# Unsplit queries for units 8 to 21, TensorE and ScalarE for the residuals of the last weight matrix, and a fourth conversion buffer

## The chip, the cores and the metric

The kernel runs on one core of a Trainium2 chip. The metric is the device time of the whole program in microseconds (us). The kernel before has a median of 1354.19 us over 3 runs (1353.14 to 1354.83).

## What is computed

Top-32 attention followed by two feed-forward layers, all in float32 accuracy:

```python
# attention: 4 batches, 8 heads, 576 positions, head size 64
scores = q @ k.T / 8
kth    = 32nd largest score of each row
attn   = softmax(scores where scores >= kth)
x      = (attn @ v), heads side by side            # 2304 x 512
# layer 1 (w_in 512x2048, w_out 2048x512)
h = x @ w_in
P = a0 + a1*h + a2*h*h + a3*h*h*h
Q = 1 + |b0|*|h| + |b1|*h*h
x = (P / (Q + 1e-6)) @ w_out
# layer 2 (w_in 512x2048, w_out 2048x512)
h = x @ w_in
y = (h * cos(h)) @ w_out                           # 2304 x 512
```

## The kernel before

**Split operands.** The matrix products of the layers use the fast 4-byte format of TensorE (`F32R`), which keeps fewer bits than float32. Each operand is therefore split: a high part (the value copied into `F32R`) and a low part (the value minus the high part), and three products high·high, high·low and low·high are summed. A product that is written with plain float32 operands appears in the profile as two matmul records.

**Weights.** The four weight matrices come in float32 and are split on the chip by `conv` (lines 264 to 312) in 64 pieces of 128x512, 16 of each kind: kind 0 and 1 are layer 1's input and output weights, kind 2 and 3 those of layer 2. The host hands them over as 8-byte words, of which a piece is loaded into a buffer `raw`. Two ScalarE instructions take the words apart into `cb` and the first half of `raw`; VectorE shifts `cb`; GpSimd adds the two (the value is now in `cb`); ScalarE copies it into the high part `h` (a resident tile, or a buffer `ch` for kind 3). Then the difference value minus high part replaces `cb`. It is made in one of three ways: for kinds 0 and 2 (`CPE`) TensorE multiplies the value by the identity and the high part by minus the identity into the PSUM tile `diff`, and ScalarE copies the sum back to `cb`; for kind 3 (`SUBV`) VectorE subtracts; for kind 1 GpSimd subtracts. At last `cb` (for kind 3 also `ch`) is written out by SyncE's DMA queue, and later matmuls stream it back. Buffers of the second phase (kinds 2 and 3): `RB` = 3 of `raw`, `CB` = 3 of `cb`. At most `CD` = 3 conversions are open at a time, and a `cb` buffer is free again only when its write has landed.

**Attention.** The work is 72 units; a unit is 128 query rows of one pair of heads. `qk` (lines 325 to 351) makes the scores of a unit in the PSUM tile `sx` and ScalarE copies them to `sS`; `topk` finds the 32nd largest with VectorE (maximum, minimum, MAX8, MATCH_REPLACE) and masks the exponentials; `av` transposes and multiplies by v. Keys are kept as high and low part stacked on the 128 partitions. Units 0 to 7 multiply the raw float32 q of 64 partitions. From unit 8 on q is split too: `high_q` (ScalarE, before the grouped stage), `low_q` (GpSimd there), and `qk` issues two `F32R` matmuls for each of the 4 score blocks of a unit.

**Order.** The program is written as pieces: piece 5u+p is step p of unit u. Units 0 to 19 (`U0` = 20) and the end are put in order by a scheduler with a timing model of its own, engine by engine; the result is a fixed order on each engine, and an engine whose next instruction waits holds everything behind it. Units 20 to 71 are "grouped": `InOrder` (lines 90 to 117) pins the order that `unit` (lines 877 to 963) writes out by hand. Layer 1 of the first 256 tokens starts at unit 9, and all 64 conversions must be done before the last step of layer 1's first block (line 703). So the conversions of layer 2's weights lie in units 8 to 19, beside attention and layer 1.

In the profile every engine instruction has line 80, the recording helper; tiles tell them apart: `cb<-cb,ch` is the subtraction of kind 3, `cb<-cb` the shift, `cb<-raw` the first ScalarE step, `cb<-diff` the copy from PSUM, `q<-qr` the high part and `q<-qr,q` the low part of q, `sx<-k,q` the split scores, `sx<-kraw,qr` the unsplit ones, `h` and `y` layer 1's products.

Of the kernel before, what the change touches and what calls it, by code (L numbers as in the profile page):

```python
# [10 lines left out]
F32 = mybir.dt.float32  # L11
# [25 lines left out]
NG = NF // 2  # L37
SINB = 2
UA, UB = 9, 18
RA, CA, RB, CB = 5, 6, 3, 3  # L40
PL = 10
P0 = 9
WIN = 8
# [9 lines left out]
WA, PA = 12, 90  # L53
WG, PG = 10, 90
N1, NU, N2, NST, NGG = 1, 2, 2, 4, 3
SUBV = (3,)
CPE = (0, 2)
LAL, LAT = 3, 10
DV1, DV2 = 8, 7
KB, VB, XB = 2, 2, 2  # L60
# [1 line left out]
QRB, QB = 2, 2  # L62
S0 = 46
U0, U1 = 20, 72
C0, C1 = 5 * U0, 5 * U1

ORDER = mybir.DependencyInfo(mybir.DependencyClass.NoSync, mybir.DependencyReason.DATA)
# [52 lines left out]
def body(tc, out, qt, kt, vt, ident_d, w1_d, w1o_d, a_d, b_d, w2_d, w2o_d):  # L120
    nc = tc.nc
    V, A = InOrder(tc, nc.vector, WIN, C0), InOrder(tc, nc.scalar, WA, PA)
    G = InOrder(tc, nc.gpsimd, WG, PG, behind=V)
    PE, SP = InOrder(tc, nc.tensor, 0, 0), nc.sync

    with ExitStack() as ctx:
# [27 lines left out]
        nu = len(units)  # L154
# [38 lines left out]
                qs_[i] = [raw, None]  # L193

        def high_q(i, grouped=False):
            if 8 <= i < nu:
                qs_[i][1] = x = att.tile([P, 2, 2, P], F32R, tag="q", bufs=QB, name=f"q{i}")
                if grouped:
                    G.tensor_copy(x[:, 0], qs_[i][0])
                else:  # L200
                    A.activation(x[:, 0], qs_[i][0], AF.Copy)

        def low_q(i, E):
            if 8 <= i < nu:
                raw, x = qs_[i]
                E.tensor_sub(x[:, 1], raw, x[:, 0].bitcast(F32))

# [56 lines left out]
        def conv(kind, c, x):  # L264
            nm = f"{kind}_{c}_{x}"
            wd = (w1_d, w1o_d, w2_d, w2o_d)[kind]
            src = wd.bitcast(I32).rearrange("(c p) (f t) -> c p f t", p=P, t=2)[c, :, x * CW:(x + 1) * CW, :]
            if kind == 2 and len(whi) == 1:
                tmps.pop().close()
                whi.append(pool("wts2").tile([P, NCC, DF], F32R, name="w2hi"))  # L270
                open_tmp()
            n1, n2 = (RA, CA) if kind < 2 else (RB, CB)
            raw = tmps[0].tmp.tile([P, CW, 2], I32, tag="raw", bufs=n1, name="raw" + nm)
            SP.dma_start(out=raw, in_=src)
            a = tmps[0].tmp.tile([P, CW], F32, tag="cb", bufs=n2, name="cb" + nm)
            lo, hi, ai = raw[:, :, 0], raw[:, :, 1], a.bitcast(I32)
            A.activation(a, hi.bitcast(F32), AF.Prelu, scale=2.0 ** -112, alpha=-2.0 ** 32)
            A.activation(lo, lo.bitcast(U32), AF.Copy, scale=2.0 ** -29)

            def rest():  # L280
                V.tensor_scalar(ai, ai, 3, 0, op0=ALU.logical_shift_left, op1=ALU.bitwise_or)
                G.tensor_add(ai, ai, lo)
                if kind == 3:
                    h = tmps[0].tmp.tile([P, CW], F32R, tag="ch", bufs=2, name="ch" + nm)
                elif kind == 1:
                    h = w1o[:, c, :]
                else:
                    h = whi[kind // 2][:, c, x * CW:(x + 1) * CW]
                A.activation(h, a, AF.Copy)
                if kind in CPE:  # L290
                    if "d" not in diff:
                        diff["d"] = ps_o.tile([P, 2, 512], F32, tag="o", name="diff")
                    diff["n"] = n = diff.get("n", 0) + 1
                    d = diff["d"][:, n % 2]
                    PE.matmul(d, ident, a, start=True, stop=False)
                    PE.matmul(d, nident, h, start=False, stop=True)
                    A.activation(a, d, AF.Copy)
                else:
                    if kind in SUBV:
                        V.tensor_sub(a, a, h.bitcast(F32))  # L300
                    else:
                        G.tensor_sub(a, a, h.bitcast(F32))
                if kind == 3:
                    SP.dma_start(out=w2o[c, :, 0, :], in_=h.bitcast(F32))
                    SP.dma_start(out=w2o[c, :, 1, :], in_=a)
                elif kind == 1:
                    SP.dma_start(out=w1ol[c], in_=a)
                else:
                    dst = wlo[kind // 2][4 * x:4 * x + 4, :, c, :].rearrange("g p t -> p g t")
                    SP.dma_start(out=dst, in_=a.rearrange("p (g t) -> p g t", t=P))  # L310

            return rest
# [8 lines left out]
        def after(mm, bank):  # L321
            for x in order[bank]:
                tc.add_manual_dep(mm.ins, x, mybir.DependencyInfo(mybir.DependencyClass.NoSync, mybir.DependencyReason.DATA), reason="bank")

        def qk(i):
            n, pr = units[i]
            raw, x = qs_.pop(i)
            hi, lo = (x[:, 0], x[:, 1]) if x is not None else (None, None)
            kvs = ins[i]
            m = P // len(kvs)  # L330
            st[i] = sb = att.tile([P, 2, S], F32, tag="sS", bufs=SB, name=f"sS{i}")
            for j in range(2):
                rows = slice(j * D, (j + 1) * D)
                for c, (k, _) in reversed(list(enumerate(kvs))):
                    qs = slice(0, (c + 1) * m)
                    for hf in range(2):
                        o = sx[qs, hf, :HALF]
                        hs = slice(hf * HALF, (hf + 1) * HALF)
                        if n < 2:
                            mm = PE.matmul(o, raw[rows, j, qs], k[rows, 0, hs].bitcast(F32), start=True, stop=True)  # L340
                            after(mm, hf)
                        else:
                            mm = PE.matmul(o, hi[:, j, qs], k[:, j, hs], start=True, stop=False, skip_group_check=True)
                            after(mm, hf)
                            mm = PE.matmul(o, lo[:, j, qs], k[:, j, hs], start=False, stop=True, skip_group_check=True)
                        order[hf] = [mm.ins.name]
                A.activation(halves(sb[:, j]), sx[:, :, :HALF], AF.Copy)
                if j == 0:
                    yield
            if n == 1:  # L350
                store_k(kvs[0][0], 0, pr)
# [417 lines left out]

        def free(i, prev):  # L770
            nq = qk(i + 1) if i + 1 < nu else iter(())
            next(nq, None)
            next(nq, None)
            if i + 2 < nu:
                load_k(i + 2)
            t = topk(i) if i < nu else iter([None] * 9)
            fresh = []
            for p in range(5):
                if p == 0:
                    for x, a in held:  # L780
                        store_k(x, *a)
                    held[:] = [(prep(*a), a) for a in preps.get(i, [])]
                    if prev is not None:
                        next(prev)
                    next(t, None)
                    if prev is not None:
                        next(prev)
                    next(t, None)
                    if prev is not None:
                        a = av(i - 1)  # L790
                        next(a)
                        next(a, None)
                        if i % 4 == 0:
                            nrm.append(norm((i - 1) // 8, (i - 1) // 4 % 2))
                            next(nrm[-1])
                            next(nrm[-1])
                            fresh.append(nrm[-1])
                    if 0 < i < nu:
                        load_v(i)
                    low_q(i + 2, G)  # L800
                else:
                    next(t, None)
                if p == 1:
                    if i + 1 < 8:
                        load_q(i + 3)
                    if i + 2 >= 8:
                        load_q(i + 4)
                if p == 2:
                    high_q(i + 3)
                if fresh and p == 1:  # L810
                    next(fresh.pop())
                if len(nrm) == 2 and p in (1, 4):
                    for x in nrm[:1] if p == 1 else nrm[1:]:
                        next(x)
                        next(x, None)
                    if p == 4:
                        nrm.clear()
                if i == U0 - 1 and p == 4:
                    for _ in qk(i + 2):
                        pass  # L820
                    load_k(i + 3)
                yield t

        def close(f, x):
# [204 lines left out]
```

## Time and profile before

| | |
|---|---|
| median of 3 runs | 1354.19 us (1353.14 to 1354.83) |
| profiled execution | 1353.97 us, of which the span shown is 1352.2 us |
| busy over the span | TensorE 91%, VectorE 87%, ScalarE 81%, GpSimd 43% |
| chain that ended last | TensorE 66%, VectorE 15%, ScalarE 9%, DMA 4% |

The shares over the whole span hide stages. The grouped stage and the end, from about 342 us on, are one stage; the first 342 us, with the conversions, are another. The rows below take the span apart at 126 us (about where unit 8 starts), 229 us (about where the conversions of layer 2's output weights start) and 342 us.

### The profile page before, as it was taken

How to read it: one execution, taken by the hardware profiler on the slowest of the kernel's cores; microseconds unless marked ns; L12 is line 12 of the kernel's file. 1: busy time of each engine (PE TensorE's matmuls, PEld its weight loads, DVE VectorE, ACT ScalarE, POOL GpSimd, SP SyncE). 2: the span in 40 equal slices, each digit the busy share in tenths (PEclk: the TensorE clock that was granted, in tenths of full speed). 3: DMA queues.
4: the chain of work that ended last, by engine and by line, in shares of the span. 5: the costliest groups of instructions: out<-in, count | busy, mean ns of one | idle time of the engine just before them, and what ended most of it. 6: DMA issues, size and time to landing. Idle time of an engine off the chain costs nothing.

```text
span 1352.2 us, 25052 instructions
## 1 busy us (share of the span) xinstructions
PE 1229.5 (91%) x8944; PEld 1095.0 (81%) x8944; DVE 1172.1 (87%) x2514; ACT 1093.1 (81%) x1869; POOL 586.1 (43%) x483
## 2 busy tenths in 40 slices
PE   6676678575899999999999999999999999999998
PEld 3343556565889998999989999999999999999996
DVE  6999879899889999999999999999999998855643
ACT  7878788775688988888898888888888888887753
POOL 2657564544245444544445554445444444430000
PEclk9677789787999999999999999999999999999999
DMA  8987777893256777766777776676667788867774
GB/s 262 327 266 225 218 239 218 273 321 140 94 161 218 234 237 253 225 202 210 234 241 243 237 227 208 212 228 205 207 214 273 261 285 284 316 232 231 237 265 155
DMA packets 155949, 314.99 MB, mean 233 GB/s; under 512 B 12592, under 2 KB 47536, under 8 KB 155824
## 3 DMA queue, kind: packets, MB, share of 16 engines
q1 hardware_dynamic: 122832, 261.99, 59.0%
q10 hardware_dynamic: 32992, 51.39, 11.8%
q8 instruction: 71, 1.16, 0.4%
q14 instruction: 54, 0.44, 0.1%
HBM read 278.20 MB, written 35.13 MB: 232 GB/s over the span
## 4 chain that ended last, share of the span: by engine, by line
PE 66%; DVE 15%; ACT 9%; DMA 4%; issue 3%; POOL 3%; ACTq 0%; DVEq 0%; POOLq 0%
PE h L80 26%; PE o L80 13%; PE y L80 12%; PE sx L80 10%; DVE e L80 7%; DVE hd L80 4%; DVE cb L80 2%; ACT r L80 1%; DVE u L80 1%; DMA w2lo<-cb 1%; ACT e L80 1%; ACT sS L80 1%; POOL q L80 1%; ACT cb L80 1%; DMA raw<-w2o 1%
## 5 line engine op out<-in xcount | busy, mean ns | idle before, releaser
L80 DVE MAX8 hd<-e 128x8 f32<-128x288 f32 (+1 forms) x576 | 320.8, 596 | 0.0
L80 PE MATMUL y<-gg,w1o 128*128 128x256 f32 x1152 | 228.1, 297 | 23.6 <-ACT gg L80 10.7
L80 POOL TENSOR_TENSOR gg<-rr,gg 128x512 fp32r<-128x512 f32 x56 | 72.4, 1292 | 400.5 <-DVE rr L80 185.7
L80 DVE MATCH_REPLACE8 e<-hd,e 128x288 f32<-128x288 f32 (+1 forms) x432 | 230.8, 540 | 0.0
L80 PE MATMUL o<-w2o,gg 128*128 128x512 f32 x864 | 223.5, 398 | 0.0
L80 PEld LDWEIGHTS y<-gg,w1o 128*128 128x128 f32 x1152 | 192.3, 203 | 28.2 <-ACT gg L80 13.3
L80 PEld LDWEIGHTS o<-w2o,gg 128*128 128x128 f32 x864 | 153.8, 189 | 26.8 <-DVE gg L80 0.3
L80 PE MATMUL h<-xh,w1hi 128*128 128x256 f32 x576 | 172.8, 300 | 1.5 <-ACT pt20a L80 1.0
L80 PE MATMUL y<-gg,w1ol 128*128 128x256 f32 x576 | 169.2, 294 | 0.0
L80 PE MATMUL h<-xl,w1hi 128*128 128x256 f32 x576 | 166.3, 289 | 2.3 <-DVE xl L80 2.3
L80 PE MATMUL h<-xh,lo 128*128 128x256 f32 x576 | 165.4, 287 | 0.0
L80 PE MATMUL h<-x2l,w2hi 128*128 128x256 f32 x576 | 162.9, 283 | 0.0
L80 PE MATMUL h<-x2h,lo 128*128 128x256 f32 x576 | 162.7, 283 | 0.0
L80 PE MATMUL h<-x2h,w2hi 128*128 128x256 f32 x576 | 162.6, 283 | 0.0
L80 DVE TENSOR_TENSOR e<-sS 128x576 f32<-128x576 f32 x144 | 117.5, 854 | 39.6 <-POOL q L80 27.7
L80 POOL TENSOR_TENSOR cb<-cb,raw 128x512 int32<-128x512 int32 x64 | 91.5, 1436 | 102.5 <-DVE cb L80 82.6
L80 DVE SCALAR_TENSOR_TENSOR e<-sS,hd,e 128x576 f32<-128x576 f32 x144 | 123.7, 887 | 3.5 <-ACT e L80 1.9
L80 PEld LDWEIGHTS h<-xh,w1hi 128*128 128x128 f32 x576 | 113.1, 196 | 13.2 <-issue 5.9
L80 PE MATMUL sx<-k,q 128*128 128x288 f32 (+1 forms) x576 | 108.4, 316 | 15.0 <-ACT xs L80 9.6
L80 PEld LDWEIGHTS h<-xl,w1hi 128*128 128x128 f32 x576 | 113.0, 196 | 5.9 <-DVE xl L80 3.8
L80 PEld LDWEIGHTS y<-gg,w1ol 128*128 128x128 f32 x576 | 117.3, 204 | 0.4 <-issue 0.3
L80 ACT ACTIVATE e<-sS,nb 128x576 f32<-128x576 f32 x144 | 105.4, 770 | 11.7 <-DVE hd L80 9.8
(1024 smaller groups left out, 3262.6 us busy)
## 6 DMA issues: line engine op xcount, KB each, us to landing
w2o<-w2o SPq DMA_DIRECT2D x144, 512.0 KB, 4.2
lo<-w1lo SPq DMA_DIRECT2D x72, 512.0 KB, 3.8
w1ol<-w1ol SPq DMA_DIRECT2D x72, 512.0 KB, 4.6
lo<-w2lo SPq DMA_DIRECT2D x72, 512.0 KB, 4.5
k<-kdr ACTq DMA_DIRECT2D x44, 576.0 KB, 5.5
raw<-w SPq DMA_DIRECT2D x32, 512.0 KB, 4.9
v<-vt ACTq DMA_DIRECT2D x48, 320.0 KB, 4.3
qr<-qt ACTq DMA_DIRECT2D x72, 128.0 KB, 2.5
```

What stands on the lines that cost most here:

```text
L80: r = f(*a, **k)
```

## The change

Three edits. (1) `QH` = 22 takes the place of unit 8 in `high_q` and `low_q`: units 8 to 21 no longer split q, and `qk` multiplies the raw q in float32, as one matmul for each of the 4 score blocks. The loads of q move: in units 0 to 19 step 1 loads q three units ahead; the first split unit (22) is prepared at the end of unit 19. (2) The difference of kind 3 is made by TensorE and ScalarE as for kinds 0 and 2. (3) `CB` = 4.

```diff
-RA, CA, RB, CB = 5, 6, 3, 3
+RA, CA, RB, CB = 5, 6, 3, 4
...
-SUBV = (3,)
-CPE = (0, 2)
+CPE = (0, 2, 3)
...
+QH = U0 + 2
...
         def high_q(i, grouped=False):
-            if 8 <= i < nu:
+            if QH <= i < nu:
...
         def low_q(i, E):
-            if 8 <= i < nu:
+            if QH <= i < nu:
...
                     A.activation(a, d, AF.Copy)
                 else:
-                    if kind in SUBV:
-                        V.tensor_sub(a, a, h.bitcast(F32))
-                    else:
-                        G.tensor_sub(a, a, h.bitcast(F32))
+                    G.tensor_sub(a, a, h.bitcast(F32))
...
+                        elif i < QH:
+                            mm = PE.matmul(o, raw[:, j, qs], k[:, j, hs].bitcast(F32), start=True, stop=True)
+                            after(mm, hf)
...
-                    low_q(i + 2, G)
...
-                if p == 1:
-                    if i + 1 < 8:
-                        load_q(i + 3)
-                    if i + 2 >= 8:
-                        load_q(i + 4)
-                if p == 2:
-                    high_q(i + 3)
+                if p == 1 and i < U0:
+                    load_q(i + 3)
...
                     load_k(i + 3)
+                    high_q(i + 3)
+                    load_q(i + 4)
```

What the fixed orders become: on VectorE, before, in units 13 and 14 (`cb_2_0` and so on are pieces of kind 3; `e`, `sS` and `hd` belong to top-32, `u_4` and `q_4` to layer 1):

```order
L80 MATCH_REPLACE e_1918<-hd_1919,e_1918 128x576 x2
L80 TENSOR_SCALAR cb_1_0_1694<-cb_1_0_1694 128x512
L80 TENSOR_TENSOR cb_1_0_1694<-cb_1_0_1694,ch_1_0_1832 128x512
L80 MAX hd_1919<-e_1918 128x8 x2
L80 TENSOR_SCALAR cb_2_0_1769<-cb_2_0_1769 128x512
L80 TENSOR_SCALAR cb_3_0_1827<-cb_3_0_1827 128x512
L80 SCALAR_TENSOR_TENSOR e_1918,sum_1026<-sS_1704,hd_1919,e_1918 128x576 x2
L80 TENSOR_TENSOR cb_2_0_1769<-cb_2_0_1769,ch_2_0_1884 128x512
L80 MATCH_REPLACE e_2108<-hd_2109,e_2108 128x288 x2
```

and on VectorE now, around the same pieces:

```order
L80 TENSOR_SCALAR cb_1_0_1652<-cb_1_0_1652 128x512
L80 MAX hd_1874<-e_1873 128x8
L80 SCALAR_TENSOR_TENSOR u_3_1771<-q_3_1769,u_3_1771 128x512
L80 MATCH_REPLACE e_1873<-hd_1874,e_1873 128x576 x2
L80 TENSOR_SCALAR cb_2_0_1722<-cb_2_0_1722 128x512
L80 MAX hd_1874<-e_1873 128x8 x2
L80 TENSOR_TENSOR e_2064<-sS_1865 128x2x288 x2
```

The subtractions `cb<-cb,ch` are gone from VectorE; the shifts `cb<-cb` stay, now with top-32 and layer 1 work between them.

On TensorE, before, at the scores of unit 15 (`w2hi` is the high part of kind 2, `pt12` and `v` belong to unit 12's product with v):

```order
L80 MATMUL sx<-pt12b,v_0_1763 64x128
L80 MATMUL diff<-cb_2_3_1567,ident 128x512
L80 MATMUL diff<-w2hi,nident 128x512
L80 MATMUL sx<-k_0_1715,q_1841 128x288 x4
L80 MATMUL diff<-cb_3_3_1663,ident 128x512
L80 MATMUL diff<-w2hi,nident 128x512
L80 MATMUL y_1636<-gg_0_3_2034,w1o 128x256
L80 MATMUL sx<-k_0_1715,q_1841 128x288 x4
```

and on TensorE now, at the second half of the scores of the same unit (`e_1873` is unit 13's):

```order
L80 MATMUL h_0_5_2124<-xh_1067,lo_0_5_1804 128x256
L80 MATMUL diff<-cb_3_0_1782,ident 128x512
L80 MATMUL diff<-ch_3_0_1858,nident 128x512
L80 MATMUL sx<-k_0_1669,qr_1738 128x288 x2
L80 MATMUL diff<-cb_4_0_1834,ident 128x512
L80 MATMUL diff<-ch_4_0_1917,nident 128x512
L80 MATMUL y_1594<-gg_0_4_2182,w1o 128x256
L80 MATMUL sx<-ident,e_1873 128x128
```

The scores are two float32 matmuls a half instead of four `F32R` ones, and the differences of kind 3 stand between the blocks of layer 1. From unit 20 on the order on every engine is the same in both kernels, but for the names of buffers.

## Rows read from the trace of the kernel before

**Rows 1.** Busy time by stretch: us, engine busy (instructions), granted TensorE clock, DMA.
```profile
core 0: us, PE busy (x) PEld busy (x) DVE busy (x) ACT busy (x) POOL busy (x), PEclk, DMA share, GB/s
...
126.00:229.00 103.00, 75.09 (x433) 57.36 (x432) 87.90 (x182) 83.11 (x159) 55.35 (x40) 0.87 0.71 217
229.00:342.00 113.00, 73.28 (x429) 64.13 (x428) 103.43 (x207) 78.33 (x146) 52.10 (x40) 0.76 0.70 235
342.00:476.00 134.00, 129.39 (x1038) 119.84 (x1037) 121.64 (x272) 114.39 (x195) 57.41 (x49) 1.00 0.57 182
476.00:1176.00 700.00, 695.88 (x5567) 646.54 (x5566) 655.61 (x1477) 607.62 (x1023) 335.87 (x286) 1.00 0.72 237
```

**Rows 2.** VectorE's waits, 126 to 342 us: total us, times, longest.
```profile
DVE cb L80 <- ACT cb L80: 15.1, 7, 3.8
DVE cb L80 <- ACT ch L80: 8.0, 5, 2.5
```

**Rows 3.** VectorE's groups, 126 to 345 us: busy us, mean ns, idle before.
```profile
L80 DVE TENSOR_TENSOR cb<-cb,ch 128x512 f32<-128x512 f32 x16 | 17.5, 1092 | 8.2 <-ACT ch L80 8.0
```

**Rows 4.** The tile cb by form: duration ns minimum/median/maximum, first and last start.
```profile
L80 POOL TENSOR_TENSOR cb<-cb,raw x64: 1283/1307/1817, 19.1 to 313.0; 128x512 int32<-128x512 int32 x64
...
L80 DVE TENSOR_TENSOR cb<-cb,ch x16: 678/888/1833, 239.9 to 318.7; 128x512 f32<-128x512 f32 x16
```

**Rows 5.** The chain that ended last, 150 to 250 us: start us, us, what.
```profile
169.17 4.50 DMA w2lo<-cb
...
185.30 2.82 DMA w2lo<-cb
...
190.72 5.65 DMA raw<-w
...
205.50 4.55 DMA w2lo<-cb
```

**Rows 6.** ScalarE's waits, 126 to 342 us.
```profile
ACT raw L80 <- DMA raw<-w2o: 6.9, 7, 2.6
ACT cb L80 <- DMA w2lo<-cb: 4.9, 6, 2.1
...
ACT raw L80 <- DMA raw<-w: 3.3, 5, 1.8
```

**Rows 7.** GpSimd's groups, 100 to 345 us.
```profile
L80 POOL TENSOR_TENSOR q<-qr,q 128x256 fp32r<-128x256 f32 x14 | 12.9, 922 | 3.4 <-ACT q L80 3.3
```

**Rows 8.** ScalarE's groups, 100 to 345 us.
```profile
L80 ACT ACTIVATE cb<-diff 128x512 f32<-128x512 f32 x20 | 11.8, 592 | 0.4 <-PE diff L80 0.2
...
L80 ACT ACTIVATE q<-qr 128x256 fp32r<-128x256 f32 x14 | 5.7, 407 | 0.0
```

**Rows 9.** TensorE in order of time: start us, us, instruction, count.
```profile
58.72 1.91 PE L80 MATMUL diff<-cb,ident 128*128 128x512 f32 x2
59.65 1.42 PE L80 MATMUL diff<-w1hi,nident 128*128 128x512 f32 x1
60.99 2.29 PE L80 MATMUL sx<-kraw,qr 64*128 64x288 f32 x4
...
122.44 1.10 PE L80 MATMUL diff<-cb,ident 128*128 128x512 f32 x2 [0.26 <-ACT cb L80]
122.98 0.79 PE L80 MATMUL diff<-w1hi,nident 128*128 128x512 f32 x1
...
264.10 1.33 PE L80 MATMUL sx<-k,q 128*128 128x288 f32 x4 [0.74 <-ACT sS L80]
```

**Rows 10.** TensorE's waits, 126 to 342 us.
```profile
PE y L80 <- ACT gg L80: 10.7, 6, 4.4
PE sx L80 <- ACT xs L80: 8.7, 8, 4.3
PE y L80 <- POOL gg L80: 7.6, 4, 3.0
PE y L80 <- DVE x2l L80: 5.3, 1, 5.3
```

## The prediction

> **What bounds the kernel now.** I read the busy time by stretch first. From 476 us to 1176 us TensorE is busy 695.88 of 700 us at full granted clock, and from 342 to 476 us 129.39 of 134 [rows 1]: there the kernel is bound by TensorE, and no edit touches an instruction of it but the scores of units 20 and 21, which are issued before. From unit 20 on the orders are the same, so what the first 342 us become shorter or longer, the whole becomes. In that first stage the picture is another: from 126 to 342 us, 216 us, VectorE is busy 87.90 + 103.43 = 191.3, ScalarE 83.11 + 78.33 = 161.4, TensorE 75.09 + 73.28 = 148.4 and GpSimd 107.5 [rows 1]. VectorE is the bound, with 216 - 191.3 = 24.7 us idle.
>
> Next I asked what VectorE waits for there. 15.1 us in 7 waits are shifts that wait for ScalarE's first step of a conversion, 8.0 us in 5 waits are kind 3's subtractions that wait for the high part [rows 2]; together 23.1 of the 24.7. The chain of waits tells what stands behind the first: three pieces of 4.50, 2.82 and 4.55 us in which the writing of an old `cb` buffer lands, and one of 5.65 us in which a raw piece is loaded [rows 5]. ScalarE itself waits 4.9 us for such landings, and 6.9 + 3.3 = 10.2 us for raw pieces [rows 6].
>
> **The change part by part.** I sum over the profiled execution, 1353.97 us, of which the span is 1352.2; that is 0.2 us from the median of 1354.19, so a difference holds for both.
>
> *Subtractions of kind 3 leave VectorE.* Sixteen, 17.5 us in all [rows 3]. The shortest takes 0.678 us, the longest 1.833 [rows 4]; 16 x 0.678 = 10.8 us is the bare work, the other 6.7 us is time in which GpSimd reads as well, and part of that will lengthen whatever VectorE does in its place. Between 10.8 and 17.5 I take 14. Gain 14 us.
>
> *The waits before them.* 8.0 us [rows 2] leave VectorE with the instructions. The high part is now waited for by TensorE, and the copy from PSUM makes ScalarE wait for TensorE; VectorE can then be held by a late exponential or a late score copy. Bounds 0 and 8; I take 5, since the same copies for kinds 0 to 2 cost ScalarE only 0.4 us of waiting in 20 [rows 8]. Gain 5 us.
>
> *The fourth `cb` buffer.* The three landings in the chain are 11.9 us [rows 5], and VectorE's waits of that kind are 15.1 [rows 2]. With four buffers and at most three open conversions a new piece no longer needs the latest write to have landed. What is late next is the raw piece, whose three buffers stay and which ScalarE already waits 10.2 us for [rows 6]. Bounds 0 and 15; I take 6, half of the landings. Gain 6 us.
>
> *No split of q in units 8 to 21.* ScalarE loses 14 x 0.407 = 5.7 us [rows 8], GpSimd 14 x 0.922 = 12.9 us [rows 7]. GpSimd is 107.5 of 216 us busy, so its own time is hidden; what counts is how much longer VectorE's instructions are beside it. A subtraction may take 1.833 - 0.678 = 1.16 us longer [rows 4], with a GpSimd addition of 1.3 us beside it. Fourteen low parts of 0.92 us can cost VectorE between nothing and 12.9 us; I take a third, 4. Gain 4 us.
>
> The Trainium skill (SBUF — State Buffer, section "SBUF: two separate sides") states that VectorE with two SBUF inputs and GpSimd lock a shared pair of ports against each other for a whole instruction. The lengthened subtractions agree with that [rows 4]. If VectorE always stood at that lock, all 12.9 us would come back and the sum below would be about 9 us better, 1324 us; no row shows VectorE at the lock for each of the fourteen, so this stays a part of the bigger-gain case.
>
> *ScalarE's new copies.* 16 x 0.592 = 9.5 us [rows 8], against the 5.7 it loses: 3.8 us more on an engine that has 216 - 161.4 = 54.6 us free. Hidden for the most part; if that cover goes, 3.8 us. I take a cost of 2.
>
> *TensorE's new work.* A difference (two records for the value, one for the high part) runs from 58.72 to 60.99 = 2.3 us at the low clock level of 1.2 GHz, and from 122.44 to 122.98 + 0.79 = 1.3 us at 2.4 GHz [rows 9]: sixteen are 21 to 37 us. Half a unit's scores take 2.29 us as float32 and 1.33 us as `F32R` at the low level [rows 9], 0.96 more; two halves of 14 units are 27 us at the low level and, at twice the clock, about 13 at the high one. The float32 row has 64 partitions where the new ones have 128, with the same 288 columns; I take the time to go by columns. Together 34 to 64 us on TensorE. It has 216 - 148.4 = 67.6 us free there, so all of it fits, but 10.7 + 8.7 + 7.6 + 5.3 = 32.3 us of that is waiting for others in a fixed order [rows 10]. The scores of a unit are issued a unit ahead of their use, which hides their greater length; a difference stands in front of a block of `h` or `y`, and holds it when the high part is late. Bounds on the path: nothing, and 64 - 35.3 = 29 us. The granted clock of 0.87 and 0.76 of full [rows 1] means 26% and 48% of the time at the low level, so the middle of the added work is about 34 + 0.37 x 30 = 45 us, of which 10 don't fit beside the waits as they are; but those waits are for VectorE and ScalarE work that comes earlier now. I take 6.
>
> Sum: -14 - 5 - 6 - 4 + 2 + 6 = -21 us, so 1354.19 - 21 = **1333 us**. The stretch would be 195 us, with VectorE about 191.3 - 18 = 173 busy and TensorE near 148 + 45 = 193 if its clock stayed as it is. So TensorE would be as good as full, and this is only possible if its clock rises: at the high level throughout, its old work would take 148.4 x (1 - 0.37/2) = 121 us and the new 34, 155 in all. That is the tightest point of this forecast.
>
> The Trainium skill (TensorE: Matmul & The Clock Gate, Part 1, on the HAM clock gate) has it that an engine kept busy is released to the full clock and an idle one falls back to half. The stage of 1.00 with 97% busy and that of 0.76 with 65% [rows 1] agree. By that rule the new work pays part of itself back.
>
> **The rivals.**
>
> *A. The idle time moves and does not go.* Raw loads and ScalarE's queue take over where the landings were. For it: 10.2 us of raw waits, three raw buffers as before [rows 6]. Against it: the bare 10.8 us leave the busiest engine in any case. Then -10.8 + 2 + 6, with nothing for waits and ports: about -3 to -12, 1346 us.
>
> *B. All terms come at their full size.* -17.5 - 8 - 15 - 6 and no cost beside it: -46, 1308 us; TensorE's 155 us plus the 32 us of waits [rows 10] need 187 of the 216, which cuts it to -29 to -42, some 1318 us at the middle. Against it: every wait of one engine would have to go without a new one.
>
> *C. Nothing measurable.* The start of the TensorE stage hangs on something that the edits leave alone: the last conversion's landing, or the 5.3 us in which `y` waits for layer 2's input [rows 10]. Then 1354 us. Against it: the conversions themselves wait on VectorE and `cb`.
>
> *D. TensorE becomes the bound of the first stage, at the low clock level.* One mechanism: the differences of kind 3 and the longer scores stand in front of `h` and `y` in TensorE's fixed order, and the waits of 32.3 us stay. It decides from 35.3 us of added work on (67.6 - 32.3). With 45 us of it the stretch grows by 10, with 64 by 29: 1364 to 1383 us. For it: the granted clock of 0.76 just where the differences come in [rows 1]. Against it: the waits are for engines that get less to do.
>
> **How the numbers follow.** Forecast (-12 to -32): 0.52. A: 0.14. B: 0.08. C: 0.08. D: 0.18. A measurement of this kernel tells about 0.2% (2.7 us) from no change. Faster: 0.52 + 0.14 + 0.08 = 0.74; same 0.08; slower 0.18. Range: down to 1313, which leaves out the better half of B, and up to 1360, which leaves out most of D. The forecast's own range is 1322 to 1342 us.
>
> **What would show it.** Unit 20 should start its top-32 about 21 us earlier than before, and every later stage keep its length. VectorE's waits for ScalarE's first step should be near 9 us and those for `ch` be none; its busy time in units 8 to 19 should fall by 18 us. The sixteen new copies should take 0.59 us each with little wait; TensorE's granted clock before the grouped stage should be above 0.87. It is wrong if TensorE's waits for `ch` or the copy's waits for `diff` come to more than 10 us, if ScalarE's waits for raw pieces grow by what the landings lose, or if the scores come late for top-32 (VectorE waiting for `sS`).

## The result, and the profile after

The kernel after takes 1339.66 us (median of four, 1338.56 to 1340.75), the kernel before 1354.13 us beside it (median of four, 1353.14 to 1354.83). The ratio is 0.9896, with a 95% interval of 0.9875 to 0.9918: 14.1 us faster, between 11.1 and 16.9. The forecast was 1333 us, so the direction and the range hold and the gain came out a third smaller than the 21 us that were forecast. The profiled execution took 1339.15 us, with a span of 1337.4.

First the busy time by stretch of the kernel after, which answers to [rows 1]; the borders stand 14 us earlier from the second stretch's end on.

```profile
core 0: us, PE busy (x) PEld busy (x) DVE busy (x) ACT busy (x) POOL busy (x), PEclk, DMA share, GB/s
...
126.00:229.00 103.00, 77.52 (x455) 56.84 (x456) 86.89 (x190) 82.14 (x158) 50.20 (x37) 0.95 0.73 231
229.00:328.00 99.00, 82.02 (x493) 63.15 (x492) 87.46 (x178) 80.06 (x151) 44.36 (x32) 0.93 0.72 245
328.00:462.00 134.00, 127.56 (x1007) 116.86 (x1006) 122.65 (x276) 113.22 (x194) 56.01 (x48) 1.00 0.59 189
462.00:1162.00 700.00, 695.28 (x5565) 646.04 (x5565) 654.95 (x1478) 607.81 (x1023) 335.85 (x286) 1.00 0.72 237
```

The long stage is what it was, 695.28 of 700 us on TensorE. The whole difference lies ahead of it. There VectorE is busy 86.89 + 87.46 = 174.4 us where it was 191.3, and TensorE 159.5 where it was 148.4, with the new products in it: its granted clock rose from 0.87 and 0.76 to 0.95 and 0.93.

To see where in the first stage the time went, I cut it at the starts of VectorE's first addition for a unit's top-32 (`e<-sS`): units 8, 14, 16, 20 and 24. Same columns, the kernel before first, then the kernel after.

```profile
126.50:229.40 102.90, 74.99 (x433) 57.59 (x433) 87.80 (x184) 82.74 (x160) 55.59 (x40) 0.87 0.71 216
229.40:291.30 61.90, 41.79 (x247) 36.06 (x245) 54.66 (x100) 48.53 (x92) 33.08 (x24) 0.78 0.87 293
291.30:360.60 69.30, 49.69 (x336) 45.96 (x337) 62.59 (x138) 43.82 (x81) 24.37 (x20) 0.80 0.44 152
360.60:424.70 64.10, 60.08 (x489) 55.11 (x488) 59.12 (x132) 53.46 (x93) 28.72 (x25) 1.00 0.52 161
```

```profile
123.60:234.60 111.00, 80.90 (x466) 58.49 (x466) 93.75 (x202) 88.86 (x171) 52.54 (x40) 0.95 0.74 234
234.60:278.50 43.90, 36.41 (x214) 27.96 (x215) 34.30 (x70) 37.71 (x71) 21.26 (x16) 0.92 0.85 293
278.50:341.90 63.40, 54.23 (x365) 44.53 (x365) 62.60 (x130) 46.39 (x89) 24.85 (x18) 0.95 0.55 182
341.90:408.80 66.90, 62.96 (x507) 57.66 (x507) 58.59 (x133) 56.80 (x98) 29.06 (x25) 1.00 0.51 164
```

The reader sees five different answers where the prediction had one sum. Unit 8 starts 2.9 us earlier, which is not the work of the edits: up to 104 us the order on every engine is the same in both kernels, and unit 6 already starts 2.3 us earlier (93.1 us against 95.4). Executions differ by that much there: over all the traces of this case unit 8 starts between 123.4 and 127.0 us. Units 8 to 13 become 8.1 us *longer*, since conversions now run ahead into them: the first `ch` is made at 226.3 us and was made at 239.2. Units 14 and 15, which held eleven of the sixteen subtractions, fall from 61.90 to 43.90 us. Units 16 to 19 gain 5.9. Units 20 to 23 lose 2.8. Together -15.9 us at unit 24, of which 13.0 arise from unit 8 on, and the end is 14.8 us earlier.

Next VectorE's waits of the kernel after, 126 to 328 us (total us, times, longest), which answer to [rows 2].

```profile
DVE cb L80 <- ACT cb L80: 13.2, 6, 6.5
DVE u L80 <- POOL u L80: 6.5, 2, 4.3
DVE e L80 <- PE sx L80: 6.0, 7, 1.8
```

The 8.0 us for `ch` are gone with their instructions, as said. But the waits for ScalarE's first step fell only from 15.1 to 13.2, and two new ones of 6.5 and 6.0 us stand in the list. From unit 8 to unit 20 VectorE is busy 190.7 of 218.3 us, where it was 205.1 of 234.1: its idle time there went from 29.0 to 27.6. So nearly all of the gain is work taken off VectorE, and next to none is waiting.

ScalarE's waits, answering to [rows 6], show the raw pieces as before, 10.7 us against 10.2, and the landings of a `cb` buffer nearly gone.

```profile
ACT raw L80 <- DMA raw<-w2o: 6.4, 3, 2.7
...
ACT raw L80 <- DMA raw<-w: 4.3, 6, 1.5
...
ACT cb L80 <- DMA w2lo<-cb: 0.9, 2, 0.7
```

In the kernel before these landings were 4.9 us for kind 2 [rows 6] and, for kind 3:

```profile
ACT cb L80 <- DMA w2o<-cb: 2.2, 1, 2.2
```

In the chain that ended last, from 150 to 250 us, two landings of `cb` are left of three, with 10.4 us in place of 11.9 [rows 5]. Over the whole stage, from 150 us on, the kernel before has four landings (15.0 us) and three raw pieces (16.0 us) in its chain, the kernel after two (10.4) and four (21.2): raw pieces take the landings' place.

```profile
166.13 4.73 DMA raw<-w
...
189.69 5.99 DMA raw<-w
...
217.98 3.83 DMA w2lo<-cb
...
224.87 6.54 DMA w2lo<-cb
...
263.50 6.40 DMA raw<-w2o
...
285.33 4.08 DMA raw<-w2o
```

Last the groups of the kernel after that answer to [rows 3, 8, 9]: ScalarE's copies from PSUM and TensorE's new products, from unit 8 to unit 20 (busy us, mean ns, idle before), and TensorE's largest wait from 126 to 328 us.

```profile
L80 ACT ACTIVATE cb<-diff 128x512 f32<-128x512 f32 x34 | 20.1, 590 | 1.2 <-PE diff L80 1.2
```

```profile
L80 PE MATMUL sx<-k,qr 128*128 128x288 f32 x96 | 28.8, 423 | 0.9 <-ACT sS L80 0.9
L80 PE MATMUL diff<-ch,nident 128*128 128x512 f32 x16 | 13.6, 853 | 0.0
```

```profile
PE diff L80 <- ACT cb L80: 10.9, 10, 2.6
```

The copies cost what was said, 590 ns each with 1.2 us of waiting in 34. TensorE's wait of 10.9 us in 10 is for ScalarE's copy of an earlier difference out of `diff`, whose two halves are used in turn; the kernel before has 4.3 us of it in 4. But 8.9 of the 10.9 lie ahead of 231 us, where only kinds 0 and 2 are made this way; behind it, where the new differences stand, it is 2.0 us in 3.

### The profile page after: what moved, and what is told of

It is laid out like the page before. It is cut to its first block, busy times and chain, and to the rows that moved or that the text cites. A ratio compares the mean times of both kernels' runs of the same rounds, so it can differ in the third digit from the quotient of the medians.

```text
span 1337.4 us, 25132 instructions
## 1 busy us (share of the span) xinstructions
PE 1233.8 (92%) x8992; PEld 1086.7 (81%) x8992; DVE 1156.0 (86%) x2498; ACT 1093.7 (82%) x1871; POOL 569.6 (43%) x469
## 4 chain that ended last, share of the span: by engine, by line
PE 62%; DVE 13%; ACT 12%; DMA 4%; issue 4%; POOL 3%; ACTq 1%; SPq 0%; POOLq 0%; DVEq 0%
PE h L80 24%; PE o L80 12%; PE sx L80 10%; PE y L80 10%; DVE e L80 6%; DVE hd L80 3%; ACT r L80 2%; DVE u L80 2%; DMA raw<-w 1%; ACT sS L80 1%; ACT e L80 1%; ACT cb L80 1%; PE diff L80 1%; DVE cb L80 1%; ACT u L80 1%
## 5 line engine op out<-in xcount | busy, mean ns | idle before, releaser
L80 PE MATMUL y<-gg,w1o 128*128 128x256 f32 x1152 | 216.1, 286 | 7.0 <-ACT gg L80 4.5
L80 PEld LDWEIGHTS y<-gg,w1o 128*128 128x128 f32 x1152 | 182.6, 193 | 12.5 <-ACT gg L80 7.1
L80 PE MATMUL y<-gg,w1ol 128*128 128x256 f32 x576 | 164.0, 285 | 0.0
L80 POOL TENSOR_TENSOR cb<-cb,raw 128x512 int32<-128x512 int32 x64 | 88.2, 1383 | 99.7 <-DVE cb L80 75.3
L80 PEld LDWEIGHTS h<-xh,w1hi 128*128 128x128 f32 x576 | 109.6, 190 | 17.2 <-issue 5.9
L80 PEld LDWEIGHTS h<-xl,w1hi 128*128 128x128 f32 x576 | 109.9, 191 | 7.7 <-DVE xl L80 4.4
L80 PEld LDWEIGHTS y<-gg,w1ol 128*128 128x128 f32 x576 | 111.4, 193 | 0.7 <-issue 0.4
L80 PEld LDWEIGHTS h<-x2l,w2hi 128*128 128x128 f32 x576 | 110.2, 191 | 0.5 <-issue 0.2
```

What stands on the lines that cost most here:

```text
L80: r = f(*a, **k)
```

## The experiments

Each kernel was timed against runs of the kernel before on the same chip, whose medians were 1353.81 to 1354.95 us. Single runs of one kernel lay up to 5.9 us from its median in these jobs, so I go by the ratios, with their 95% intervals; a gain in us is the ratio's distance from 1 times 1354.

**One part at a time.** The new difference alone: kind 3's difference goes the way of kinds 0 and 2.

```diff
-SUBV = (3,)
-CPE = (0, 2)
+SUBV = ()
+CPE = (0, 2, 3)
```

> The kernel before with only the differences of kind 3 made by TensorE and ScalarE; q split and three cb buffers as before. Theory S (the gain is VectorE's relief from the sixteen subtractions and the waits before them; the fourth buffer and the unsplit q give little by themselves): 1342 to 1346 us, 8 to 12 us faster than before, unit 20 some 8 to 14 us earlier. Theory T (only the three edits together pay, since TensorE's copies come back late and hold the three cb buffers): within 3 us of before.

Measured: 1349.46 us, ratio 0.9963 (0.9943 to 0.9984), a gain of 5.0. The fourth buffer alone:

```diff
-RA, CA, RB, CB = 5, 6, 3, 3
+RA, CA, RB, CB = 5, 6, 3, 4
```

> The kernel before with only the fourth cb buffer. The prediction's term was 6 us of gain. Theory S: under 3 us of change, since VectorE's waits for ScalarE's first conversion step were still 13.2 us with all edits (15.1 before). Theory T: 1348 us, with those waits down to about 9 us.

Measured: 1348.05 us, 0.9945 (0.9929 to 0.9962), a gain of 7.4. VectorE's waits of this kernel, 126 to 335 us:

```profile
DVE cb L80 <- ACT cb L80: 13.8, 6, 5.2
DVE cb L80 <- ACT ch L80: 2.3, 2, 1.8
```

The waits for the first step, for which the buffer was counted, fell by 1.3 us alone; those for `ch`, which the prediction had put down to the new difference, fell by 5.7. The prediction took VectorE's 15.1 us for waits on landings; in the instruction records of the kernel before ScalarE is at work in 12.9 us of them, and a landing of `cb` holds it in 1.2. What the buffer did take is ScalarE's own waits for landings, which fell from 7.1 to 2.8 us, while its waits for raw pieces rose from 12.3 to 17.4 us (126 to 345 us).

The unsplit q alone: up to unit 21, with the scheduling of its loads as in the change, but kind 3 left on VectorE and three `cb` buffers. Against the kernel after:

```diff
-RA, CA, RB, CB = 5, 6, 3, 4
+RA, CA, RB, CB = 5, 6, 3, 3
...
-CPE = (0, 2, 3)
+CPE = (0, 2)
...
-                    G.tensor_sub(a, a, h.bitcast(F32))
+                    (V if kind == 3 else G).tensor_sub(a, a, h.bitcast(F32))
```

> The kernel before with only the unsplit q of units 8 to 21 and the moved loads of q. The prediction's term was 4 us of gain on VectorE less some 3 us on TensorE. Theory S: 1350 to 1356 us; GpSimd's shorter work is taken back by the 2.8 us that the start of the grouped stage loses when the raw q is held until its scores are done. A rival: the 13 us of GpSimd count in full, 1345 us or less.

Measured: 1351.70 us, 0.9984 (0.9968 to 1.0001), a gain of 2.2 whose interval just touches no change. The sum of the three is 14.6 where all together gave 14.1. So at the end of the program the parts add up, within these intervals, and two of the three came near their terms: 7.4 for 6, and 2.2 for the 4 less the share of the 6 that the longer scores have. The one that fell short is the largest, the new difference.

Its trace shows where. VectorE's longest wait of that kernel from 126 to 335 us, and the row of units 14 and 15:

```profile
DVE cb L80 <- ACT cb L80: 28.3, 12, 5.4
```

```profile
229.40:290.10 60.70, 48.04 (x277) 35.07 (x275) 42.83 (x89) 52.58 (x100) 29.41 (x24) 0.94 0.84 284
```

In the kernel before the subtractions of these two units are:

```profile
L80 DVE TENSOR_TENSOR cb<-cb,ch 128x512 f32<-128x512 f32 x11 | 12.1, 1099 | 7.0 <-ACT ch L80 6.9
```

VectorE's busy time there fell from 54.66 to 42.83 us, 11.8 less, so all of the 12.1 us left; and the stretch became only 1.2 us shorter: idle time grew from 7.2 to 17.9. Its waits for ScalarE's first step went from 15.1 us in 7 to 28.3 in 12. How long a piece now takes is seen on one piece of that kernel, in order of time (start us, us; the lines of the `cb` path alone):

```profile
249.85 0.64 ACT L80 ACTIVATE ch<-cb 128x512 fp32r<-128x512 f32 x1
...
252.80 0.50 PE L80 MATMUL diff<-ch,nident 128*128 128x512 f32 x1
...
256.73 0.58 ACT L80 ACTIVATE cb<-diff 128x512 f32<-128x512 f32 x1
257.34 0.32 SPq L305 DMA_DIRECT2D w2o<-cb  x1
...
259.85 0.68 ACT L80 ACTIVATE cb<-raw 128x512 f32<-128x512 f32 x1 [1.05 <-DMA w2o<-cb]
```

The same way of one piece in the kernel before:

```profile
260.50 0.62 ACT L80 ACTIVATE ch<-cb 128x512 fp32r<-128x512 f32 x1
...
261.58 0.69 DVE L80 TENSOR_TENSOR cb<-cb,ch 128x512 f32<-128x512 f32 x1
262.29 0.32 SPq L305 DMA_DIRECT2D w2o<-cb  x1
```

From the end of the high part to the end of the difference the one takes 257.31 - 250.49 = 6.8 us and the other 1.15. Over the sixteen pieces the mean, worked out from the instruction records, is 4.9 us against 1.75, and from ScalarE's first step to the finished difference 10.1 against 8.3. The work itself is 2 us; the rest is standing in TensorE's order and then in ScalarE's, where the copy of this piece starts 3.4 us after its product has ended. So the buffer is held longer, and the next first step waits 1.05 us for its writing (the last line of the first piece). But such waits are not what grew: ScalarE waits 1.8 us in 2 for landings of kind 3's `cb` in that kernel, against 2.2 in 1 before. The growth of VectorE's waits, 13.2 us, lies in five waits behind 230 us (13.0 us in all), and ScalarE is at work in 12.1 of them. The longest, with the end of ScalarE's queue ahead of it:

```profile
280.39 0.58 ACT L80 ACTIVATE cb<-diff 128x512 f32<-128x512 f32 x1
...
283.13 0.60 ACT L80 ACTIVATE cb<-diff 128x512 f32<-128x512 f32 x1 [0.35 <-PE diff L80]
283.63 0.66 ACT L80 ACTIVATE cb<-raw 128x512 f32<-128x512 f32 x1
284.32 0.43 DVE L80 TENSOR_SCALAR cb<-cb 128x512 int32<-128x512 int32 x1 [5.42 <-ACT cb L80]
```

The first step that VectorE needs stands last of nine ScalarE instructions, two of them copies from `diff`, and ScalarE is idle for 0.4 us of the 5.4. Over units 14 and 15, where the copies of ten of the sixteen new differences stand, ScalarE is busy 52.58 of 60.70 us, 87%; before it was 48.53 of 61.90, 78%. So the added waiting is ScalarE working off a fixed order with the copies in it. Whether the longer hold has a part in that order, through the scheduler's planning, no run shows.

**A third buffer for raw q.** All three edits and a third buffer for raw q. The theory was that the 2.8 us which are lost between units 20 and 24 are the load of unit 22's q, which the kernel after issues late.

```diff
-QRB, QB = 2, 2
+QRB, QB = 3, 2
```

> The changed kernel with a third buffer for raw q. Theory: after unit 20's start the changed kernel loses 2.8 us (18.7 us ahead at unit 20, 15.9 at unit 24), because the load of unit 22's q is issued only at 338.0 us, when unit 20's scores have let go of the buffer, and ScalarE waits 1.85 us for it. With a third buffer the wait goes and the time is 1336 to 1338 us. Rival: the loss is from something else there (layer 2's first phase, VectorE waiting for GpSimd's q), and the time stays at 1339 to 1341 us.

Measured: 1342.74 us, 0.9911 (0.9883 to 0.994): a gain of 12.1, no better than the kernel after. Unit 20 started at 337.5 us, 4.4 earlier than in the kernel after, and unit 24 at 413.5, 4.7 later. The load of unit 22's q now landed at 335.8 us, ahead of unit 20, and ScalarE no longer waited for it. The theory fell: the load is not what costs the 2.8 us.

**Two parts at a time.**

> Differences of kind 3 by TensorE and ScalarE together with the fourth cb buffer; q split from unit 8 on as before. Alone, the first gave 4.7 us and let VectorE's waits for ScalarE's first conversion step grow from 15.1 to 28.3 us; the second gave 6.1. Theory P (the copy coming back late holds a cb buffer, so the two belong together): more than their sum of 10.8 us, 1337 to 1341 us, with those waits back at 13 to 15 us; then the unsplit q adds nothing. Theory Q (the terms add): 1342 to 1345 us.

Measured: 1342.99 us, 0.9914 (0.9892 to 0.9937), a gain of 11.6; the singles' sum is 12.4.

> Unsplit q together with the fourth cb buffer; VectorE subtracts for kind 3 as before. Both theories: the sum of what each gave alone, 8.6 us, 1344 to 1348 us.

Measured: 1348.28 us, 0.9951 (0.9933 to 0.9969), a gain of 6.6; the sum is 9.6.

> Unsplit q together with the differences of kind 3 by TensorE and ScalarE, three cb buffers. Theory P: the long way of kind 3 meets three buffers, so little more than the 4.7 us of it alone, 1346 to 1351 us, with VectorE waiting 25 us or more for ScalarE's first step. Theory Q: 7.2 us, 1345 to 1348 us.

Measured: 1347.85 us, 0.9944 (0.9923 to 0.9965), a gain of 7.6; the sum is 7.2. Each pair is the sum of its parts within the uncertainty of some 3 us, so that one part needs another can't be told at the end of the program. In particular the fourth buffer does not make the new difference worth more there: 5.0 us with three buffers and 11.6 - 7.4 = 4.2 with four. Theory P, that the held buffer is what costs, is not borne out: VectorE's waits for the first step, where it said 13 to 15 us, are still 22.4 in the pair with four buffers (126 to 335 us):

```profile
DVE cb L80 <- ACT cb L80: 22.4, 10, 5.8
```

**Fewer unsplit units.** All three edits, but q is left unsplit in units 8 to 15 alone, and the loads of q keep the places they had before:

```diff
-QH = U0 + 2
+QH = 16
...
```

> All three edits, but q is unsplit only in units 8 to 15; from unit 16 on it is split as before. Theory: from unit 18 on TensorE is the bound (busy 0.89 to 0.98 of the time), and there the float32 scores take about 1 us a unit more at the high clock level, so leaving units 16 to 21 split gives back 3 to 6 us: 1334 to 1337 us. Rival: the ScalarE and GpSimd steps of the split cost as much there as they save, 1338 to 1342 us.

Measured: 1341.59 us, 0.9903 (0.988 to 0.9927), a gain of 13.1. Neither the longer scores of units 16 to 21 nor the moved loads cost anything that can be told.

**What the difference costs at all.** The kernel before without kind 3's subtraction: the low part is stored as the value itself, so layer 2's output weights have a wrong low part, and only the time is of use.

```diff
-                    if kind in SUBV:
-                        V.tensor_sub(a, a, h.bitcast(F32))
-                    else:
+                    if kind not in SUBV:
                         G.tensor_sub(a, a, h.bitcast(F32))
```

> The kernel before, but the difference of kind 3 is not made at all: the low part of layer 2's output weights is stored as the undiminished value, so the output is not the reference's. It shows what the sixteen subtractions cost where nothing takes their place. Theory L (VectorE's relief is worth what the prediction said, 19 us, and the new way by TensorE and ScalarE eats most of it): 1334 to 1340 us. Theory M (the relief itself is small, since VectorE then waits for the next conversion's first step): 1345 to 1349 us, with those waits above 22 us.

Measured: 1337.09 us, 0.9868 (0.9842 to 0.9895), a gain of 17.9. That is the relief that the first two terms of the prediction stand for, 14 + 5 = 19. It is not a matter of shorter holds: from ScalarE's first step to the last step on a `cb` buffer it is 8.5 us in the mean here and 8.3 before. The new way takes back 17.9 - 5.0 = 12.9 of it, and the two intervals lie far apart (0.9842 to 0.9895, 0.9943 to 0.9984).

The row of units 14 and 15 of this kernel tells where:

```profile
226.20:277.30 51.10, 34.15 (x234) 28.36 (x233) 43.83 (x91) 45.01 (x87) 30.59 (x24) 0.91 0.94 331
```

With the subtractions gone and nothing in their place ScalarE is the fullest engine there, 45.01 of 51.10 us or 88%, just ahead of VectorE's 43.83. The new way adds 7.6 us to ScalarE's work (52.58) and 13.9 to TensorE's, which has more room (48.04 of 60.70 us), and the two units become 9.6 us longer, while VectorE's work stays (42.83).

Then the same omission in the kernel after, with four buffers and q unsplit:

```diff
-CPE = (0, 2, 3)
+CPE = (0, 2)
...
-                    G.tensor_sub(a, a, h.bitcast(F32))
+                    if kind != 3:
+                        G.tensor_sub(a, a, h.bitcast(F32))
```

> The changed kernel, but the difference of kind 3 is not made at all (the undiminished value is stored as the low part, so the output is not the reference's): what the way by TensorE and ScalarE costs where four cb buffers are there. With three buffers and split q it cost 12.9 us (only_cpe against no_difference: 0.9963 and 0.9868 of before). Theory W (the copy coming back late holds the cb buffer, and the fourth buffer pays for it): the way costs 3 to 6 us here, 1334 to 1337 us. Theory X (the cost is TensorE's and ScalarE's own work in a fixed order, whatever the buffers): 10 us or more, 1330 us or less.

Measured: 1336.70 us, 0.9876 (0.9846 to 0.9906), a gain of 16.8: 2.7 more than the kernel after, with intervals that overlap. Read by the end alone the difference costs 12.9 us with three buffers and next to nothing with four, the time of theory W. The starts of the units say otherwise. Rows of units 8, 14, 16, 20 to 24 as above, for this kernel:

```profile
126.10:236.10 110.00, 78.68 (x463) 56.67 (x463) 94.78 (x202) 89.14 (x170) 51.96 (x40) 0.97 0.75 238
236.10:273.30 37.20, 27.67 (x192) 24.34 (x191) 33.82 (x69) 32.39 (x62) 22.34 (x16) 0.91 0.95 312
273.30:332.90 59.60, 46.98 (x295) 37.98 (x294) 58.11 (x129) 42.44 (x81) 24.75 (x17) 0.83 0.56 203
332.90:405.50 72.60, 70.48 (x557) 65.12 (x557) 61.65 (x137) 58.55 (x99) 30.31 (x27) 0.98 0.51 158
```

And units 20 to 23 of the kernel before without the difference:

```profile
340.10:405.30 65.20, 63.46 (x522) 59.13 (x522) 59.04 (x134) 56.20 (x97) 30.57 (x26) 1.00 0.52 171
```

Each kernel without the difference has the same order on every engine as the one with it up to 231 us or later, so I count from the start of unit 14; that leaves out by how much single executions differ before. From unit 14 to unit 20 the kernel after takes 341.9 - 234.6 = 107.3 us, and 332.9 - 236.1 = 96.8 without the difference: the new way costs 10.5 us with four buffers. With three it costs (356.5 - 229.4) - (340.1 - 226.2) = 13.2 us. So the fourth buffer pays for little of it, against theory W. Up to unit 24 the cost is 14.3 us with three buffers and 4.8 with four: it shrinks in units 20 to 23. There the kernel after without the difference has 557 TensorE products where the kernel after has 507, and TensorE is busy 70.48 of 72.60 us, 97%: what a faster stage has not yet done on TensorE it has to catch up with.

**A fourth raw buffer.** All three edits and one more raw piece in the second phase (the room for it taken by placing the split q elsewhere).

```diff
-RA, CA, RB, CB = 5, 6, 3, 4
+RA, CA, RB, CB = 5, 6, 4, 4
```

> The changed kernel with a fourth buffer for raw pieces in the second phase (the tiles of split q come from the pool that opens after the conversions, to make room). Theory M: with four cb buffers the raw pieces are late next (ScalarE waits 10.7 us for them in units 8 to 19 of the changed kernel, and four loads of 4 to 6.5 us lie in its chain of waits), so a fourth gives 4 to 8 us: 1332 to 1336 us. Rival: at most three conversions are open, the waits move to another step, 1338 to 1342 us.

Measured: 1340.15 us, 0.9879 (0.9855 to 0.9903), a gain of 16.4, against 14.1 with three raw buffers; the intervals overlap, and the time expected if the raw pieces bound the stage was not reached. Whether they cost the kernel after 2 us or nothing stays open.

**Another order.** All three edits, with one number of the planner moved so that the same instructions stand in another order, from 221 us on.

```diff
-C2 = 80
+C2 = 79
```

> The changed kernel with the conversions of the second phase started on a schedule one piece shorter (79 for 80), no work added or taken away: how much the fixed orders of the scheduler are worth by themselves. If the orders matter little, 1338 to 1341 us; if differences of a few us between edits are partly an order that happened to be good or bad, 3 to 8 us to either side.

Measured: 1341.18 us, 0.9894 (0.9869 to 0.9919): the gain of the kernel after, so one other order gives the same.

No kernel beat the one after by more than these measurements can tell, not even the two that leave work out.

## Why the prediction was right, and where its size was off

- **What bounds the kernel.** Right in the main. The long stage kept its length: -15.9 us at unit 24, -14.8 in the span. But "what the first 342 us become shorter or longer, the whole becomes" held only from unit 24 on; between units 20 and 24 2.8 us were given back.
- **Subtractions off VectorE, and their waits: 14 + 5.** Right as a relief: leaving the difference out gave 17.9 us. Of VectorE's busy time itself 11.7 us left units 8 to 19 with the new difference alone (205.05 to 193.31 us), against 17.5 of subtractions [rows 3] and the 14 that were forecast: the eleven of units 14 and 15 went in full, and in units 16 to 19, where five more had stood, it stayed at 62.6 to 62.7.
- **The failed step: "+2" for ScalarE's copies and, of the "+6" for TensorE's work, what belongs to the differences.** The prediction priced these by engine time over the whole stretch: 9.5 us of copies on an engine with 54.6 free, 21 to 37 us of products on one with 67.6 free. Together they stood at some 6 us (2 and about two thirds of 6). Measured, the new way takes back 12.9. The free time was not where the copies fell: in units 14 and 15, with eleven of the sixteen subtractions, ScalarE had 61.90 - 48.53 = 13.4 us free, and with the subtractions gone it is the fullest engine there, just ahead of VectorE (45.01 of 51.10 us); the new way added 7.6 us to it and 9.6 us to the two units. A step that was one instruction on one engine became three on two, each in a fixed order; VectorE's wait for ScalarE's first step grew by 13.2 us in the kernel with the new difference alone, with ScalarE at work in nearly all of it. The prediction had the sentence for TensorE's half ("a difference stands in front of a block of `h` or `y`, and holds it when the high part is late") but did not ask what stands behind the copies on ScalarE. A `cb` buffer was also held longer, 4.9 us after its high part (5.7 in the kernel after) instead of 1.75, but that this is what costs isn't shown: with a fourth buffer the cost at unit 20 was still 10.5 us, after 13.2.
- **The fourth buffer: 6.** Right in size, 7.4 (5.1 to 9.6) alone, and wrong in place: VectorE's waits for the first step stayed (13.8 us, and 13.2 in the kernel after, where about 9 were forecast), since ScalarE was at work in most of them, and those for `ch` went. The sum counts the `ch` waits with the new difference, which removes them too, so that term's own credit was partly the buffer's. So its size was in part luck: it came by another way than the one that was priced.
- **q unsplit: 4, less its scores.** Right within what can be told: 2.2 alone, 2.5 beside the other two (14.1 - 11.6). In the trace of that edit alone VectorE's busy time in units 8 to 19 fell by 6.4 us (205.05 to 198.62), half of the 12.9 that GpSimd was spared, and units 8 to 19 became 9.4 us shorter; 4.9 of that were given back in units 20 to 23, which took 69.0 us in place of 64.1.
- **TensorE's clock.** Right. The tightest point of the forecast was that the new work fits only if the clock rises; it rose to 0.95 and 0.93, and with it rival D fell, whose 1364 us and more needed the low level. The Trainium skill (TensorE: Matmul & The Clock Gate, Part 1) says that an engine kept busy is released to the full clock; these rows agree, 148.4 us of work at 0.87 and 0.76 against 159.5 at 0.95 and 0.93.
- **The rivals.** A (the idle time moves, 1346 us) comes near what the new difference does by itself: 1349.46. For the whole change the truth lies between A and the forecast. B and C fell. In B's working the cut to "-29 to -42" gives a reason for the 29 alone (216 - 187).
- **Signs.** Unit 20 starts 18.7 us earlier, not 21, and 2.9 of that lie ahead of unit 8. VectorE's busy time in units 8 to 19 fell by 14.4 us, not 18. Scores did come late for the top-32, which the prediction had named as a sign against it: over units 8 to 19 6.3 us, but the kernel before has 4.2 of it there. Without the difference 4.5 us are left of the 6.0 that stand in the list of waits, so most of it does not come from the differences.

What was not foreseen at all is the end of the stage. From unit 20 to 23 TensorE is busy 94% of the time before and after, and 97% in the two kernels without the difference. Of the five kernels with all three edits, four (the one after, that with four raw buffers, that in another order, that with q unsplit to unit 15) start unit 20 between 336.3 and 343.6 us, 7.3 us apart, and unit 24 between 407.3 and 410.3, 3.0 apart. The fifth, with a third buffer for raw q, starts unit 20 at 337.5 and unit 24 only at 413.5:

```profile
337.50:413.50 76.00, 73.88 (x585) 68.51 (x585) 66.03 (x148) 59.12 (x102) 31.51 (x27) 0.98 0.49 156
```

TensorE is busy 97% there too, with 585 products in units 20 to 23; the kernel before has 489, the kernel after 507, the one with four raw buffers 556. An earlier unit 20 leaves more of TensorE's work to those units, so what a faster VectorE wins at unit 20 TensorE does not follow. In the kernel after this gives back 2.8 us. I read it from these rows; no run took work off TensorE there, so it isn't tested.

## What to carry to other kernels

When a step is moved from one engine to two, price it where it lands: take the free time of those engines in the stretch where the step falls, not over a longer one, and ask what stands behind the new instructions in each fixed order. Measure the relief by leaving the step out; what the new way takes back is then one subtraction. And look at the engine that decides the next stage: how much it has to catch up with there bounds what a faster stage ahead of it can bring.

## What the runs showed of the hardware

Work that leaves VectorE need not take its contention along. The same addition `e<-sS` in units 8 to 19, in the kernel before, in the one with the new difference alone, in the kernel after, and in the kernel after in another order (busy us, mean ns):

```profile
L80 DVE TENSOR_TENSOR e<-sS 128x576 f32<-128x576 f32 x25 | 25.4, 1046 | 4.2 <-PE sx L80 4.2
```

```profile
L80 DVE TENSOR_TENSOR e<-sS 128x576 f32<-128x576 f32 x24 | 26.3, 1130 | 0.0
```

```profile
L80 DVE TENSOR_TENSOR e<-sS 128x576 f32<-128x576 f32 x24 | 26.7, 1148 | 6.3 <-PE sx L80 6.3
```

```profile
L80 DVE TENSOR_TENSOR e<-sS 128x576 f32<-128x576 f32 x25 | 23.6, 977 | 3.5 <-PE sx L80 3.3
```

Its mean rose by 84 and 102 ns with sixteen subtractions gone, and in the kernel after with GpSimd's 12.9 us of low parts [rows 7] gone as well; in the other order of the same instructions it fell by 69. In the first three kernels the addition takes 731 to 759 ns whenever no GpSimd instruction runs beside it, and up to 1855 ns beside one. Of the 24 that start in units 8 to 19 GpSimd is beside 8 in the kernel before and beside 13 in the next two. So how much of a lengthening comes back hangs on the order, and a row's mean that holds lengthening is no measure of what its removal brings: here 11.7 us of 17.5.
